# Chunk 0 of a gated linear attention with experts behind it: f and q in rows of two tokens, another order of loads, and a new table of offsets

## The chip, the cores and the metric

The kernel runs on one core of one Trainium2 chip. Its time is the device time of one execution in microseconds (us); the lower, the better. The engines are TensorE (PE, with the loading of weights shown apart as PEld), VectorE (DVE), ScalarE (ACT), GpSimd (POOL) and SyncE (SP), which here only issues transfers. L282 is line 282 of the kernel's source.

## The reference, cut to what matters

The inputs are q, k, v and f_logit of shape [4, 8, 768, 48] (batch, head, token, width) in float32. Attention is a recurrence over the tokens, with one 48x48 state for each batch and head; behind it every token of 384 values goes through four experts, whose outputs are added with the weights p.

```python
f = 1.0 / (1.0 + np.exp(-f_logit))
for t in range(S):
    state = f[:, :, t, :, None] * state + np.einsum('bhd,bhe->bhde', k[:, :, t], v[:, :, t])
    y[:, :, t] = np.einsum('bhd,bhde->bhe', q[:, :, t], state)
...
x = np.ascontiguousarray(attn_out.transpose(0, 2, 1, 3)).reshape(B * S, H * D)
p = domain_probs / (domain_probs.sum(-1, keepdims=True) + 1e-09)
for e in range(E):
    h = np.maximum(x @ w1[e], 0.0)
    out += p[:, e:e + 1] * (h @ w2[e])
```

w1 is [4, 384, 1024] and w2 is [4, 1024, 384]. The output has 3072 rows of 384.

## The kernel before

**Tiling.** The 768 tokens are cut into 6 chunks of 128, and each chunk is worked on for the 4 batches b0 to b3 one after the other; a token of the chunk is a partition. Within a chunk the recurrence is written as matrix products. With G the running sum of the gate logits (-log f) over the tokens of the chunk, q is multiplied by exp(-G) and k by exp(G); the product of the two, masked to the lower triangle, times v gives y, and from the second chunk on the carried state adds its part.

**The steps of one batch.** They have these names in the plan:

- `gate1` (L311) takes exp(-f) on ScalarE, and `gate2` (L315) takes ln(1 + that), in bfloat16, into a tile whose heads are padded to 64.
- `cs` (`pe_cs`, L319) is the running sum, one matmul of 384 columns with an upper triangle of ones (`Ub`). In chunk 0 four matmuls of a single column (L322) add up the whole chunk for the state.
- `exps` takes the two exponentials on ScalarE (L339), and in chunk 0 a small third one (L341) of the chunk's totals.
- `q` and `k` are the two products (`product`, L347), on VectorE or POOL.
- `tp` (L356) turns both with eight transposes on the PE, and `ev_tp` (L272 on ScalarE, L273 on VectorE) copies the result out of PSUM. Later chunks use a transposing transfer.
- `at` (L383) is eight matmuls of 128 columns, `ev_at0` and `ev_at1` (L387, VectorE) multiply their results by the mask `mask01` and write bfloat16 (the tile `AT`).
- `y` (L398, in later chunks also L394), then `ev_y` or `ev_ys` (L370) copies it, and `xt` (L423) turns it into the experts' input x; `ev_xt` copies that.
- `kv` (L404), `ev_kv` (L411) and `sf` (L416, L419) carry the state on.

**The experts.** The first chunks do them straight: `h` (L432) is x times w1 in blocks, `relu` (L441 or L443) cuts them off, `o` (L447) multiplies by w2 and `ev_o` adds it up with p. From the second half of chunk 1 on, two experts at a time go through a scheme that saves multiplications: `hs` (L464), `relu_s` (L470 on VectorE, L472 on ScalarE), sums of blocks `s1` to `s4` (L482), seven products `p` (L501) for each pair, `ev_p` (L509) and the stores (L513). `t` (L491) makes sums of w2 once.

**What sets the order.** The class `Plan` gives every step an engine or several to choose from, a cost, a priority, the steps it depends on, and the buffers that it takes and frees. A list scheduler walks through time, gives each free engine the first step by priority that is ready, and its answer is the fixed order in which each engine's instructions are emitted. The engines then run these lists in order, each waiting for what it needs. The table `MOVES` shifts the priority of single steps, or pins them to an engine. Until the first `h` the PE gets filler matmuls on a constant tile (L873), as many as fit into the gaps of the plan.

**Loads.** SP issues the loads of f, q, k (L282), each of one batch in chunk 0, of two batches later. The values v of chunk 0 come through POOL's queue, which casts them to bfloat16 on the way (L278). The weights come through POOL's queue too (`load_w`, L291), in eleven pieces w0 to w10: the halves of w1 of experts 0 and 1 (w0 to w3), the halves of w2 of expert 0 (w4, w5), then whole matrices: w1 of expert 2, w2 of expert 1, w1 of expert 3, w2 of experts 2 and 3. The last, w10, waits for the k of chunk 1. The order of chunk 0's loads is one line, with the places of v0 and v1 in it, each held back by one of the k loads; v2 and v3 go out behind w0:

```python
v_gate, issued = [(0, "k", 1), (0, "k", 2)], []
...
for i, x in enumerate("f0 k0 q0 f1 k1 q1 f2 f3 k2 q2 v0 k3 q3 v1".split()):
```

Each such load has a packet for each token and head, 48 values of 4 bytes. `set-up` in what follows means the constants made on POOL and VectorE before the first step: the triangle (a float32 tile `U` and its copy `Ub`), the identity, a column of ones, the zeros of the padded tiles, the mask.

Of the kernel before, what the change touches and what calls it, by code (L numbers as in the profile page):

```python
# [15 lines left out]
    "k 0.2=46.8@DVE;at 0.1=35.2;ev_xt 0.0=109.8@DVE;ev_at1 0.1=70.1;ev_y 0.3=27.8@ACT;cs 1.0=11.6;at 1.1=19.4;ev_xt 1.0=-4.1@DVE;"  # L16
    "y 1.1=-37.1;ev_ys 1.2.1.1=-9.1;ev_kv 1.3=70.1;ld q2.0=-1.5;ld k2.2=0.2;ld v2.2=15.3;relu 0.0.0.0=-7.7@DVE;h 0.0.0.256=-53.5;"
    "h 0.0.4.256=16.5;o 0.0.0.1=5.7;h 0.1.3.0=25.3;o 0.0.1.1=45.6;o 0.0.3.0=67.2;o 0.1.3.1=6.9;relu 0.3.2.0=15.9@DVE;h 0.3.3.0=-4.2;"
    "h 0.3.6.0=-15.8;o 0.2.3.0=-0.7;h 0.3.7.0=377.1;o 0.2.3.1=-2.5;tp 2.3=-3.5;at 2.1=1.3;ev_ys 2.0.0.0=-60.4@ACT;xs 2.0.1=-2.5;"
    "ev_at0 2.1=-36;ev_at0 2.2=23.5;xs 2.3.0=11.1;kv 2.0=-27.5;sf 2.0.1=-9.9;sf 2.0.3=-58.7;ld f3.0=3.2;o 0.3.1.1=10.5;o 0.3.3.0=-6.7;"  # L20
    "o 0.3.3.1=-22.1;store 0.3.0=20.5;h 1.1.3.0=2.6;o 1.0.1.1=-1;h 1.2.4.0=8.1;h 1.2.5.0=43.5;h 1.3.0.0=-9.1;o 1.2.0.0=19.1;"
    "relu 1.3.1.0=-6.8@ACT;o 1.2.1.0=1.8;h 1.3.3.0=10.5;relu 1.3.7.0=7@DVE;hs 1.1.1.0.0=-39.6;hs 1.1.1.0.4=-28.6;egs 3.1=26.2;"
    "tp 3.1=-56.1;q 3.2=2.6;ev_at0 3.1=7.2;ev_ys 3.1.0.1=20.9;ev_kv 3.0=13.3;kv 3.2=18.7;kv 3.3=10.8;ld q4.0=-7;ld k4.2=14.4;"
    "p 1.1.1.5=-1.3;ev_p 1.1.1.5=-31.6;store 1.2.0=32.2;p 1.1.1.4=5.8;s1 2.0.0=-10.2;hs 2.0.1.0.0=7;relu_s 2.0.1.0.4=1.8@ACT;"
    "p 2.0.0.4=-14.9;s1 2.0.1=2.2;hs 2.1.0.0.0=-31.7;ev_p 2.0.1.1=-60.4;ev_p 2.0.1.2=4.7;hs 2.1.0.0.2=-47.5;relu_s 2.1.0.1.2=2.4@ACT;"
    "hs 2.1.0.0.4=0.4;p 2.0.1.7=10.9;ev_p 2.0.1.3=-15.8;hs 2.1.0.1.6=-2.8;s1 2.1.0=-39.4;s2 2.1.0=2.3;p 2.1.0.1=1.8;p 2.1.0.2=56.5;"
    "ev_p 2.1.0.6=-15.4@DVE;p 2.1.0.5=-1.9;hs 2.1.1.1.6=-3;relu_s 2.1.1.1.6=9.4@DVE;s3 2.1.1=-18;cs 4.0=-6.9;egs 4.0=1.1;q 4.0=0.6;"
    "v 4.1=-4.6;tp 4.1=-14.2;cs 4.2=-65.6;cs 4.3=-4.7;ev_ys 4.0.0.1=-2.9@DVE;ev_ys 4.1.1.0=-89;ev_ys 4.2.1.1=0@ACT;ev_at0 4.3=55.1;"
    "ev_kv 4.1=52.4;kv 4.2=12.3;ld k5.0=7.4;ld f5.2=7.3;ld k5.2=-22.8;hs 3.0.0.0.2=1.4;relu_s 3.0.0.0.2=0@ACT;p 2.1.1.6=17.2;"
    "p 2.1.1.4=17.3;s4 3.0.0=8.2;relu_s 3.0.1.1.0=31.3@DVE;ev_p 3.0.0.2=-39.3;relu_s 3.0.1.0.2=36.2@DVE;p 3.0.0.5=2.3;hs 3.0.1.0.4=2.5;"  # L30
    "relu_s 3.0.1.1.4=8.8@ACT;p 3.0.0.4=3.4;hs 3.0.1.1.6=-5.6;relu_s 3.0.1.1.6=-12.6@DVE;p 3.0.1.1=7.7;hs 3.1.0.1.0=4.3;p 3.0.1.2=0.6;"
    "hs 3.1.0.0.4=-3.5;hs 3.1.0.1.6=2.1;s1 3.1.0=-4.1;s2 3.1.0=-28.8;s3 3.1.0=13.5;hs 3.1.1.0.0=0.4;relu_s 3.1.1.0.0=0@DVE;"
    "hs 3.1.1.1.0=-32.5;hs 3.1.1.1.2=5.9;relu_s 3.1.1.0.4=6.7@DVE;s1 3.1.1=10.8;s2 3.1.1=-19.8;gate1 5.2=-24.6;cs 5.2=-43.5;cs 5.3=10.3;"
    "ev_at0 5.0=-17.9;ev_at1 5.0=-18.3;ev_ys 5.0.0.0=0.1@DVE;ev_ys 5.0.0.1=18.3@DVE;ev_ys 5.1.0.0=-2.7@DVE;ev_ys 5.1.1.0=31.5@DVE;"
    "ev_at1 5.3=45.4;hs 4.0.0.0.0=23.1;hs 4.0.0.1.0=2;hs 4.0.0.0.4=-0.9;hs 4.0.0.1.4=-2.8;p 3.1.1.3=31;hs 4.0.0.0.6=-1.9;"
    "hs 4.0.0.1.6=-58.1;s2 4.0.0=6.2;hs 4.0.1.0.0=24.8;hs 4.0.1.1.0=-11.5;ev_p 4.0.0.7=-23.6;hs 4.0.1.0.6=-26.6;ev_p 4.0.0.4=2.3@DVE;"
    "hs 4.0.1.1.6=49.8;hs 4.1.0.0.2=-81.9;s1 4.1.0=-16.7;s2 4.1.0=-21.4;s4 4.1.0=-5.2;ev_p 4.1.0.1=-31.4@DVE;hs 5.0.1.1.2=15.3;"
    "hs 5.0.1.0.4=-23.8;hs 5.1.0.0.2=40.5;hs 5.1.0.1.4=9.9;hs 5.1.1.1.6=18;p 5.1.0.5=15.2"
# [3 lines left out]
class Op:  # L42


    def __init__(self, name, costs, emit, prio, deps=(), takes=(), frees=(), lag=0.0):
        self.name, self.costs, self.emit, self.prio = name, costs, emit, prio
        self.deps = [d for d in deps if d is not None]
        self.takes, self.frees, self.lag = list(takes), list(frees), lag
        self.end = self.start = self.engine = None
        self.pad = 0  # L50
        self.port, self.turn = False, None


class Plan:
# [37 lines left out]
    def run(self):  # L92
# [3 lines left out]
        for o in self.ops:  # L96
            if o.name.split(" ")[-1].startswith("0.") and set(o.costs) & {"ACT", "DVE"}:
                o.lag += 0.1
# [41 lines left out]
def kernel(  # L140
# [11 lines left out]
    nc = tc.nc  # L152
# [36 lines left out]
    U = const.tile([T, T], FP32)  # L189
    make_upper_triangular(nc, U, val=1.0, diag=True)  # L190
    Ub = const.tile([T, T], BF16)
    nc.gpsimd.tensor_copy(out=Ub, in_=U)
    ident = const.tile([T, T], BF16)
    make_identity(nc, ident)
    ones = const.tile([T, 32], BF16, name="ones")[:, 0:1]
    nc.gpsimd.memset(ones, 1.0)
    pads = {}
    for nm, nb in (("gp", 2), ("qk", 2)):
        for i in range(rooms[nm]):
            t = pads[nm, i] = const.tile([T, nb, H, P2], BF16, name=f"{nm}{i}")  # L200
            nc.vector.memset(t[:, :, :, D:P2], 0.0)
    for i in range(rooms["e"]):
# [710 lines left out]
```

## Time and profile before

| | |
|---|---|
| median of 3 runs | 289.22 us (288.99 to 289.73) |
| the profiled execution | 288.44 us |
| its span, first to last instruction | 286.7 us |
| granted TensorE clock | 1.000 |
| PE busy | 280.0 us, 98% of the span, 3010 matmuls |
| VectorE, ScalarE, POOL busy | 195.5, 180.7, 112.0 us |
| transferred | 41.85 MB in 157782 packets, 148124 of them under 512 bytes |

The page of the profile gives totals over the span and the span in 40 slices. Engines that are busy less than the whole span may still be what the others wait for in one stage, so the stages are read one by one: a view of windows gives each engine's busy time between two moments, the chain of waits says what ended last before each piece of the path, and the timeline of one engine lists its operations with the idle time ahead of them and what ended it. A row of the timeline reads: start, duration, engine, line, operation, output and inputs, count, and in square brackets the idle time before it and the releaser.

### The profile page before, as it was taken

To read this page: it belongs to the slowest core of one execution; us is meant where nothing else is said; L and a number is where in the kernel's file an instruction comes from. 1 tells how busy PE (TensorE), PEld (TensorE's weight loads), DVE (VectorE), ACT (ScalarE), POOL (GpSimd) and SP (SyncE) were. 2 spreads that over 40 slices of the span, in tenths; PEclk is the share of its full clock that TensorE was granted. 3 is DMA by queue.
4 is the path that set the end of the run, shared out by engine and by line. 5 is a ranking of instruction groups with operands and counts; after the bars stand their busy time and mean duration, and the time that the engine had idled before them with its cause. 6 is when DMAs were issued, how large, how long until landed. Compare 5 with 4: busy or idle time off the path is not lost.

```text
span 286.7 us, 7475 instructions
## 1 busy us (share of the span) xinstructions
PE 280.0 (98%) x3010; PEld 235.7 (82%) x3016; DVE 195.5 (68%) x385; ACT 180.7 (63%) x343; POOL 112.0 (39%) x181
## 2 busy tenths in 40 slices
PE   7999999999999999999999999999999999999994
PEld 2567555567786999998999999999999999998994
DVE  4595122778698868846889876888885787630683
ACT  5847683758776846867695657375865544659500
POOL 5796500218763762478157258134373000000000
PEclk9999999999999999999999999999999999999999
DMA  7999999997998989999889999995254143420011
GB/s 154 206 173 206 207 195 201 181 198 167 176 184 161 213 154 211 128 222 195 177 182 171 126 219 179 222 184 112 58 132 90 28 84 83 88 56 2 2 55 55
DMA packets 157782, 41.85 MB, mean 146 GB/s; under 512 B 148124, under 2 KB 156956, under 8 KB 157748
## 3 DMA queue, kind: packets, MB, share of 16 engines
q1 hardware_dynamic: 146500, 34.66, 63.7%
q0 software_dynamic: 11248, 6.72, 16.5%
q8 instruction: 23, 0.38, 0.6%
q14 instruction: 11, 0.09, 0.1%
HBM read 31.51 MB, written 4.72 MB: 126 GB/s over the span
## 4 chain that ended last, share of the span: by engine, by line
PE 93%; SPq 2%; DMA 2%; DVE 1%; issue 0%; ACT 0%; DVEq 0%
PE ps_m L464 33%; PE ps_m L501 29%; PE ps_m L447 11%; PE ps_m L432 11%; SPq L282 2%; PE ps_m L383 2%; PE ps_m L398 2%; DMA q<-in_q_dram 2%; PE ps_m L394 1%; PE ps_m L404 1%; PE ps_m L319 1%; PE ps_m L356 1%; DVE AT L387 0%; ACT QK L272 0%; PE ps_m L423 0%
## 5 line engine op out<-in xcount | busy, mean ns | idle before, releaser
L464 PE MATMUL ps_m<-x,w_sb 128*128 128x256 bf16 x864 | 105.6, 273 | 0.0
L472 ACT ACTIVATE h<-ps_m 128x512 bf16<-128x512 f32 x113 | 67.2, 598 | 45.3 <-PE ps_m L464 35.9
L464 PEld LDWEIGHTS <-w_sb 128*128 128x128 bf16 x864 | 82.9, 98 | 9.1
L501 PEld LDWEIGHTS <-S 128*128 128x128 bf16 x576 | 48.6, 98 | 1.1
L509 DVE TENSOR_TENSOR o<-ps_m,o 128x192 f32<-128x192 f32 x91 | 31.2, 354 | 20.0 <-PE ps_m L501 17.7
L482 DVE TENSOR_TENSOR S<-h 128x1024 bf16<-128x1024 bf16 x36 | 28.2, 800 | 13.0 <-ACT h L472 12.9
L501 PEld LDWEIGHTS <-h 128*128 128x128 bf16 x432 | 36.3, 98 | 0.9
L447 PE MATMUL ps_m<-w_sb,h 128*128 128x384 bf16 x192 | 36.1, 326 | 0.0
L432 PE MATMUL ps_m<-x,w_sb 128*128 128x128 bf16 (+2 forms) x260 | 35.6, 281 | 0.2
L443 ACT ACTIVATE h<-ps_m 128x512 bf16<-128x512 f32 (+1 forms) x49 | 24.6, 512 | 14.0 <-PE ps_m L432 12.9
L387 DVE TENSOR_TENSOR AT<-ps_m,mask 128x512 bf16<-128x512 f32 x48 | 30.5, 683 | 4.1 <-PE ps_m L383 3.8
L419 POOL TENSOR_TENSOR Sf<-Sf,egs 48x192 f32<-48x192 f32 x40 | 20.7, 521 | 28.4 <-DVE Sf L411 23.9
L339 ACT ACTIVATE e<-ps_m 128x384 f32<-128x384 f32 x48 | 26.9, 671 | 6.3 <-PE ps_m L319 2.9
L470 DVE TENSOR_SCALAR h<-ps_m 128x512 bf16<-128x512 f32 x31 | 21.0, 691 | 12.9 <-PE ps_m L464 10.3
L432 PEld LDWEIGHTS <-w_sb 128*128 128x128 bf16 x264 | 21.8, 98 | 9.4
L347 POOL TENSOR_TENSOR qk<-q,e 128x384 bf16<-128x384 f32 x19 | 24.1, 1271 | 13.7 <-ACT e L339 6.3
L501 PE MATMUL ps_m<-ts_sb,S 128*128 128x192 bf16 x288 | 28.7, 246 | 0.0
L501 PE MATMUL ps_m<-w_sb,S 128*128 128x192 bf16 x288 | 28.5, 246 | 0.0
L501 PE MATMUL ps_m<-w_sb,h 128*128 128x192 bf16 x288 | 28.4, 246 | 0.0
L447 PEld LDWEIGHTS <-h 128*128 128x128 bf16 x192 | 18.3, 98 | 11.9 <-issue 0.4
L370 ACT ACTIVATE yb<-ps_m,pn 128x384 bf16<-128x384 f32 x49 | 26.1, 584 | 2.8 <-PE ps_m L398 2.7
L347 POOL TENSOR_TENSOR qk<-k,e 128x384 bf16<-128x384 f32 x19 | 19.4, 1023 | 14.7 <-DVE Sf L411 4.0
(74 smaller groups left out, 308.7 us busy)
## 6 DMA issues: line engine op xcount, KB each, us to landing
out_dram<-o SPq DMA_DIRECT2D x23, 192.0 KB, 2.2
w_sb<-in_moe_w_dram POOLq DMA_DIRECT2D x5, 768.0 KB, 17.3
k<-in_k_dram SPq DMA_DIRECT2D x10, 384.0 KB, 5.5
q<-in_q_dram SPq DMA_DIRECT2D x10, 384.0 KB, 5.6
v<-in_v_dram SPq DMA_DIRECT2D x10, 384.0 KB, 5.6
f<-in_f_logit_dram SPq DMA_DIRECT2D x9, 384.0 KB, 4.9
w_sb<-in_moe_w_dram POOLq DMA_DIRECT2D x6, 384.0 KB, 8.7
f<-in_f_logit_dram SPq DMA_DIRECT2D x6, 192.0 KB, 3.8
```

Source lines behind the costliest of these rows:

```text
L339: nc.scalar.activation(out=o, in_=i, func=AF.Exp, scale=1.0 if j else -1.0)
L347: return engines[eng].tensor_tensor(out=tl("qk", c, b)[:, j, :, 0:D].rearrange("t (i r) d -> t i r d", r=2), in0=tl("qk"[j], c, b // 2)[:, ...
L370: nc.scalar.activation(out=ys, in_=y, func=AF.Copy, scale=pe)
L387: nc.vector.tensor_tensor(out=tl("AT", c, b)[:, r].rearrange("s i t -> s (i t)"), in0=tl("A", c, b, r).rearrange("s i t -> s (i t)"), in1= ...
L432: nc.tensor.matmul(out=hp(c, e, fc, n0, n1, nf)[:, f], lhsT=w1_sb[:, e, kk, (fc + f) * 128:(fc + f + 1) * 128], rhs=tl("xT", c)[:, kk, n0: ...
L443: nc.scalar.activation(out=dst, in_=src, func=AF.Relu)
L447: nc.tensor.matmul(out=tl("op", c, e, nt, part)[:, cols], lhsT=tl("h", c, e, half_of(c, nt * T))[:, fc, nt * T:(nt + 1) * T], rhs=w2_sb[:, ...
L464: nc.tensor.matmul(out=out_[:, f], lhsT=w1_sb[:, e, kk, (fc + f) * 128:(fc + f + 1) * 128], rhs=tl("xs", c, hf, p)[:, el, kk, :], start=(k ...
L472: nc.scalar.activation(out=dst, in_=tl("hp", c, hf, p, el, fc), func=AF.Relu)
L482: return nc.vector.tensor_tensor(out=s(j), in0=in0, in1=in1, op=op)
L501: nc.tensor.matmul(out=out_, lhsT=lhs[:, fc, :], rhs=rhs[:, fc, :], start=(first and fc == 0), stop=(fc == KF - 1), skip_group_check=True)
L509: nc.vector.tensor_tensor(out=o, in0=src, in1=o, op=ALU.add)
```

## The change

- f and q of chunk 0 are loaded with two consecutive tokens in one row: partition 2p+g holds the tokens 2p and 2p+1 for the heads of group g, so a packet has 384 bytes, and a load half as many of them. The eight loads concerned are named by `PAIRED`. k and v stay as they were.
- The running sum of chunk 0 is made twice, since q and k now lie differently. `pe_cs`, for k, is four matmuls of 192 columns with a new constant `Up`, and eight single-column ones with the constant `par`. The new `pe_cq`, for q, is four matmuls of 192 columns with `Wp`, in a PSUM tile of its own (`cq`). The exponential of q (`expq`) is a step of its own. The q product writes the padded tile by group, and the masked matmul (`pe_at`) reads its right side and writes its result with a stride, so that the tokens stand in order again.
- The set-up makes `par` (a reduction on VectorE), `Up` (four selects on POOL) and `Wp` (two copies on VectorE); `U` and its copy are gone, `Ub` is made directly, and the mask is bfloat16 instead of float32.
- The order of chunk 0's loads is written in `ORDER`, that of the v loads and weights in `SEQ`, what holds v0 and v2 back in `GATE`. The emitted order on SP is f0, q0, the probabilities, f1, f2, k0, q1, k1, f3, k2, q2, q3, k3; on POOL v0 (behind f1), v1, v2 (behind k2), the product k of b2, w0, v3, w1 and the further pieces.
- All of `MOVES` is replaced. Among the rest, the first load of chunk 2's f is now emitted on SP ahead of the last q and v loads of chunk 1.
- The plan's extra 0.1 of lag for chunk 0's steps moves into the class `Op`, and a few costs are set anew.

```diff
...
-    "k 0.2=46.8@DVE;at 0.1=35.2;ev_xt 0.0=109.8@DVE;ev_at1 0.1=70.1;ev_y 0.3=27.8@ACT;cs 1.0=11.6;at 1.1=19.4;ev_xt 1.0=-4.1@DVE;"
...
+    "ld k0.0=1.9;ld f0.2=-2.8;ld q0.2=5.3;ld q0.3=33.8;ld k0.3=74.5;w 5=-5.3;exps 0.0=4.4;ev_tp 0.0=12.5@ACT;cs 0.1=-7.1;expq 0.2=68;"
...
-    U = const.tile([T, T], FP32)
-    make_upper_triangular(nc, U, val=1.0, diag=True)
-    Ub = const.tile([T, T], BF16)
-    nc.gpsimd.tensor_copy(out=Ub, in_=U)
...
+    par = const.tile([T, 32], BF16, name="par")[:, 0:2]
+    nc.vector.tensor_reduce(out=par, in_=ident.rearrange("c (p g) -> c g p", g=2), axis=mybir.AxisListType.X, op=ALU.max)
+    Up = const.tile([T, 2, 2, T], BF16)
+    Wp = const.tile([T, 2, T], BF16)
+    for j in range(2):
+        for g in range(2):
+            nc.gpsimd.affine_select(out=Up[:, j, g], in_=par[:, g:g + 1].broadcast_to([T, T]), compare_op=ALU.is_ge, fill=0.0,
+                                    base=g - j, channel_multiplier=-1, pattern=[[1, T]])
+    Ub = const.tile([T, T], BF16)
+    nc.gpsimd.memset(Ub, 1.0)
+    nc.gpsimd.affine_select(out=Ub, in_=Ub, compare_op=ALU.is_ge, fill=0.0, base=0, channel_multiplier=-1, pattern=[[1, T]])
...
+    for j in range(2):
+        nc.vector.tensor_copy(out=Wp[:, j].rearrange("c (p g) -> c g p", g=2),
+                              in_=Up[:, j].rearrange("c g (p i) -> c g p i", i=2)[:, :, :, 0])
...
-    mask01 = const.tile([T, NP * T], FP32)
+    mask01 = const.tile([T, NP * T], BF16)
...
-            if b < 2:
-                after(ins[c, nm, b], ins[v_gate[b]])
+            if f"v{b}" in GATE:
+                after(ins[c, nm, b], ins[GATE[f"v{b}"]])
+            return
+        if c == 0 and nm in PAIRED:
+            src = {"f": f_logit, "q": q}[nm][b, :, 0:T, :].rearrange("(g h) (p j) d -> p g h (j d)", g=2, j=2)
+            ins[c, nm, b] = nc.sync.dma_start(out=tl(nm, c, b // 2)[:, hh(b), :].rearrange("t (h j) d -> t h (j d)", j=2), in_=src)
             return
...
     def gate2(c, b, n):
         g = tl("gp", c, b // 2).rearrange("t b h d -> t (b h) d")
+        if c == 0:
+            nc.scalar.activation(out=g[:, hh(b), 0:D].rearrange("t (j h) d -> t h j d", j=2),
+                                 in_=tl("f", c, b // 2)[:, hh(b), :].rearrange("t (h j) d -> t h j d", j=2), func=AF.Ln, bias=1.0)
+            return
...
-        nc.tensor.matmul(out=cs[:, 0:HD], lhsT=Ub, rhs=g[:, :, 0:D], start=True, stop=True)
-        if c == 0:
-            for i in range(NP):
-                nc.tensor.matmul(out=cs[:, HD + i:HD + i + 1], lhsT=flat(g, i), rhs=ones, start=True, stop=True)
+        if c > 0:
+            nc.tensor.matmul(out=cs[:, 0:HD], lhsT=Ub, rhs=g[:, :, 0:D], start=True, stop=True)
+            return
+        for r in range(2):
+            for j in range(2):
+                nc.tensor.matmul(out=cs[:, r * HD // 2:(r + 1) * HD // 2], lhsT=Up[:, j, r], rhs=g[:, 4 * j:4 * j + 4, 0:D],
+                                 start=(j == 0), stop=(j == 1), skip_group_check=True)
+        for i in range(NP):
+            for j in range(2):
+                nc.tensor.matmul(out=cs[:, HD + i:HD + i + 1], lhsT=flat(g, j * 2 + i % 2), rhs=par[:, i // 2:i // 2 + 1],
+                                 start=(j == 0), stop=(j == 1), skip_group_check=True)
+
+    def pe_cq(b):
+        g, cs = tl("gp", 0, b // 2)[:, b % 2], tl("cq", 0, b)
+        for r in range(2):
+            for j in range(2):
+                nc.tensor.matmul(out=cs[:, r * HD // 2:(r + 1) * HD // 2], lhsT=Wp[:, int(j > r)], rhs=g[:, 4 * j:4 * j + 4, 0:D],
+                                 start=(j == 0), stop=(j == 1), skip_group_check=True)
...
         if c == 0:
+            nc.scalar.activation(out=tl("e", c, b)[:, 2 * NP * P2:], in_=cs[:, 0:HD], func=AF.Exp, scale=1.0)
             nc.scalar.activation(out=tl("egs", c, b)[0:MP, 0:NP], in_=cs[0:MP, HD:HD + NP], func=AF.Exp, scale=-1.0)
+
+    def expq(b):
+        nc.scalar.activation(out=tl("e", 0, b)[:, 0:HD], in_=tl("cq", 0, b)[:, 0:HD], func=AF.Exp, scale=-1.0)
...
+        if (c, j) == (0, 0):
+            return engines[eng].tensor_tensor(out=tl("qk", c, b)[:, 0, :, 0:D].rearrange("t (j h) d -> t j h d", j=2),
+                                              in0=tl("q", c, b // 2)[:, hh(b), :].rearrange("t (h j) d -> t j h d", j=2),
+                                              in1=tl("e", c, b)[:, 0:HD].rearrange("t (j h d) -> t j h d", j=2, d=D), op=ALU.mult)
...
+                if c == 0:
+                    qt = QK[rows, 0].rearrange("m (j i) (p g) -> m i g p j", i=2, g=2)[:, i % 2, i // 2]
+                    a = a.rearrange("t (p j) -> t p j", j=2)
+                nc.tensor.matmul(out=a, lhsT=QK[rows, 1, i, :], rhs=qt, start=True, stop=True)
...
+PAIRED = "fq"
+ORDER = "f0 q0 k0 f1 q1 k1 f2 f3 q2 k2 q3 k3"
+SEQ = "v0 v1 v2 w0 v3 w1"
+GATE = {"v0": (0, "f", 1), "v2": (0, "k", 2)}
+LATE = {}
```

## The prediction

> **What bounds the kernel now.** I read the page first: the row of granted clock says one speed throughout, and the PE row is full from the third of 40 slices on. Then the stages:
>
> ```profile
> span 286.7 us, 7475 instructions
> ...
> PE   7999999999999999999999999999999999999994
> ...
> PEclk9999999999999999999999999999999999999999
> ```
>
> ```profile
> core 0: us, PE busy (x) PEld busy (x) DVE busy (x) ACT busy (x) POOL busy (x), PEclk, DMA share, GB/s
> 0.00:20.38 20.38, 17.50 (x164) 9.62 (x166) 12.75 (x28) 12.22 (x28) 14.59 (x29) 1.00 1.23 176
> 20.38:283.20 262.82, 262.51 (x2847) 226.03 (x2851) 182.19 (x357) 168.50 (x317) 97.45 (x153) 1.00 0.78 144
> 283.20:286.70 3.50, 0.00 (x0) 0.00 (x0) 0.57 (x2) 0.00 (x0) 0.00 (x0) 1.00 0.24 84
> ```
>
> From 20.38 to 283.2 the PE idles 0.31 us; before that much of its busy time is filler (matmuls of L873 on a constant tile, 32 in the records). After it come 3.5 us of last sums and stores. So the time is: when chunk 0's attention hands the PE its work, plus a fixed amount of matmuls, plus whatever waits a new order puts in, plus the tail. What sets 20.38 is in the chain of waits and in VectorE's timeline:
>
> ```profile
> 8.20 4.64 DMA q<-in_q_dram
> ...
> 12.93 0.57 DVE qk L347
> ...
> 17.16 1.08 ACT QK L272 x2
> ...
> 19.03 1.30 DVE AT L387 x2
> ...
> 20.38 0.35 PE ps_m L398 x7
> ```
>
> ```profile
> 10.10 1.28 DVE L387 TENSOR_TENSOR AT<-ps_m,mask 128x512 bf16<-128x512 f32 x2
> 12.93 0.56 DVE L347 TENSOR_TENSOR qk<-q,e 128x384 bf16<-128x384 f32 x1 [1.55 <-DMA q<-in_q_dram]
> 13.40 0.55 DVE L347 TENSOR_TENSOR qk<-k,e 128x384 bf16<-128x384 f32 x1
> ...
> 16.59 1.88 DVE L387 TENSOR_TENSOR AT<-ps_m,mask 128x512 bf16<-128x512 f32 x3
> ...
> 19.03 1.29 DVE L387 TENSOR_TENSOR AT<-ps_m,mask 128x512 bf16<-128x512 f32 x2 [0.30 <-PE ps_m L398]
> ```
>
> The third batch's q lands at 12.84, VectorE waits 1.55 us for it, then works nearly without a stop to 20.32: loads to 12.9, VectorE from there. Steps below are "b0" to "b3", the batches of chunk 0.
>
> **The change, part by part.**
>
> *Loads.* In the window 3 to 7 us queue 1 moved 4569 packets, all of 192 bytes, at a share of 111.3% of 16 engines: 1.113 x 16 x 4.0 / 4569 = 15.6 ns each, so 1024 of them take 1.0 us of the 16 engines. Rows of two tokens make 512 packets of 384 bytes. The trace has no such packet. The stores between 280 and 287 us average 47 ns at 1024 bytes (432 packets, 16.6%, the 48 small ones taken off at 8 ns); a line through both gives 23 ns for 384 bytes, an estimate, 0.73 us a load. Bounds: 31 ns (two small ones, nothing gained) and 15.6 ns (half the time). Eight loads (f and q) at 0.27: 2.1 us less in the stream, with 0 and 4.0 as ends. f of b0 lands at 3.25 rather than 3.52. The values v0 and v1 now go out once f1 is in (about 5.4 to 7.2 on POOL, 1.06 and 0.95 each) instead of at 7.61 and 11.42, and share the engines with q1 to k3. Between 9 and 12 us the one v load cost the others about 0.8 us, so k3, now the last, lands near 14, against 14.87 for the last q before. It is needed at 15.4 (below): loads stop being what VectorE waits for.
>
> *ScalarE.* Per batch two gates (0.53, 0.52), two exponentials (0.87 for two), one small (0.18): the same five, in another order. Nothing.
>
> *TensorE before the masks.* Per batch one 384-column matmul and four of one column become eight of 192 and eight of one. Early matmuls start 0.43 us apart for 512 columns, 0.16 for 192; later 0.21, and 0.083 for 192 (L501 rows: 8 in 0.66). Single columns take 0.065 (3 weight loads in 0.20). So cq is 0.64 then 0.35, cs 1.15 then 0.85. In program order from the end of gate2 b0 (3.25 + 1.1 = 4.35): cq0 0.64, cs0 1.15, the four transposes of the probabilities 0.8, a filler 0.3 (7.25); cs1 0.85, tpq0 0.22, cq1 0.35, filler 0.21, tpk0 0.22, cq2 0.35, cs2 0.85, filler, tpk1, filler, tpq1 0.9: 11.2. With 0.15 of latency and the copy of QK1 on VectorE (0.6; it starts back-to-back operations that much apart) the first mask AT0 begins at about 12.0; I take 12.2 for the joins. Ends: 11.4 (the array fast from the start) and 13.7 (a rival).
>
> *VectorE from there.* AT0 1.22, q2 0.47, AT1 1.22, q3 and k3 0.94, the copy of y0 0.42, AT2 1.22, x0 0.30, half of AT3 0.61, x1 0.30, the other half 0.61: 7.3 us, to 19.5, when the y of b3 may start; it ends at 19.9. Before it ended at 20.73. The copy of x1 stands at 18.9 in this list, so the PE has by 19.9 also done the h block of b1 (0.65) and the transposes of b2 (0.15), which before came after 20.73. Gain: 0.83 + 0.65 + 0.15 = 1.6 us. POOL now multiplies one k only (0.99 to 1.00 each before), beside VectorE operations that read PSUM. The bf16 mask is read beside f32 from PSUM: taken as no change, at best 0.05 each.
>
> *Set-up.* POOL has four selects of 0.29 and two operations on Ub instead of U's two and its cast: it ends near 5.4 instead of 3.9. Its first user is v0, gated by f1 at 4.8: 0.6 late, needed at 15. VectorE adds a reduction (0.25) and two copies (0.23) and is ready at 5.1; its first product is due at 5.8. If that cover went, each 0.1 would move the product, which has 0.5 to spare before k0.
>
> *Weights.* The first piece now stands in POOL's queue behind v2's issue (gated by k2, near 11) and the product of k2 (needs exps2, 11.0): issued near 13 instead of 12.37. Behind it wait v3 and all other pieces. Before, v1 landed at 15.93 and this piece 2.4 us later; now three v are through by about 15, so it lands at 17.3 (18.33 before). Its user, h of b0, can start at 18.1. The second piece lands near 19.9 (21.79), wanted at 20.6. Later pieces follow 1.9 us apart, 1.9 us earlier than before, and the PE wants them 1.6 earlier. Cost nothing; covers of 0.8 and 0.7 us.
>
> *New offsets.* From 20.4 on the PE's instructions are the same in another order. At most the 0.31 idle can go; at the other end every wait in an in-order queue counts in full. I take 0: counted over the new order, blocks stand behind the operations that feed them about as before.
>
> *Tail.* Two sums of the last-but-one pair's group now come last and one more store of 192 KB: 0.2 (0 to 0.7), from 0.36 for an issue and 0.31 for a sum.
>
> Sum: -1.6 + 0 + 0.2 = -1.4. The profiled execution took 288.44 with a span of 286.7, and stands 0.78 below the median of 289.22; the difference goes on both: span 285.3, 287.0 for a like execution, 287.8 for the median.
>
> **The rivals.**
>
> *A, more.* The single-column matmuls and the early ones run faster than I put them, AT0 starts at 11.4, and the new order saves the idle 0.3: -2.5, 286.7. For it: three single-column weight loads show 0.20 while the array is slow. Against: the PE list then must have no join in it.
>
> *B, the array stays slow.* The row of granted clock shows 1.00 from the start, yet L873 starts 0.43 us apart until 6.8 and 0.21 apart later. The new program has 21 fillers instead of 34, and single-column matmuls in their place. If the switch comes late, the column time of cs1 to tpq1 doubles: (0.64 + 0.64 + 0.85 + 0.6) = 2.8 us at most, about 1.4 if it comes half-way. AT0 then starts at 13.6 and the gain is gone: 289.2. Against: the PE still has work from 1.5 us on. The Trainium skill, page "TensorE: Matmul & The Clock Gate", section "Part 1: The HAM clock gate", has the array at half clock until one free-running window of about 3.4 us was busy; by that rule the switch comes at a window's end, near 6.9 or, missed, 3.4 us later, which is this rival; the trace agrees on the factor of two and not in the granted-clock row.
>
> *C, slower: a late weight piece in the dense stage.* The last piece (w2 of expert 3) waits for chunk 1's k, issued at 49.59, landed 9.1 us later at 58.67; its matmuls began at 59.79. They now come up near 58.2. SyncE's list has a 384 KB load more (chunk 2's f, 2048 packets, 2.0 us) ahead of chunk 1's last q and v, in just that stretch. If the pieces do not move earlier and this load goes ahead, it lands at 60.7, a stall of 2.5: +1.1, 290.3. It turns the sign once it lands after 59.6. Against: everything ahead of it on the engines is 2.1 us less, so 56.6 is as good a guess, and the load waits for a buffer. The same price holds wherever the new order meets a late operand.
>
> **How the numbers follow.** The likeliest, 287.8 (own range 287.0 to 288.7): 0.46. A 0.18, B 0.14, C 0.22. 0.3% is 0.87 us, about what a measurement of this kernel can tell from no change. Faster takes A and nine tenths of the likeliest: 0.59. Same: the rest of it and most of B: 0.17. Slower: C and a little of B: 0.24. Range 286.0 to 290.8: below A by the 0.7 that packets at 15.6 ns could add, above C by the tail's upper end.
>
> **What would show it.** Right: queue 1 in the first 12 us at about 23 ns for a packet; no wait of VectorE for a load after 6 us; AT0 near 12.2 and unbroken work behind it to 19.5; two h blocks before the y of b3; PE idle from there to the end below 0.7 us. Wrong: AT0 after 13 with early matmuls still 0.16 apart for 192 columns (B); a PE gap over 0.5 us beside a weight piece's landing (C) or behind another engine; a first h block that waits for its weights; a tail over 4 us.

## The result, and the profile after

The changed kernel takes 290.14 us (median of 20 runs, 289.42 to 291.50), the kernel before 289.05 (20 runs beside them, 288.27 to 290.63): a ratio of 1.0039, 95% interval 1.0027 to 1.0052. It is slower by 1.1 us, where 1.4 us less was forecast. The profiled execution took 289.52 us, with a span of 287.7. The page, and the stages in the view of windows, cut where the y of b3 ends (22.55) and where the last matmul ends (283.80):

```profile
span 287.7 us, 7539 instructions
...
PE   6999999999999999999999999999999999999994
...
PEclk9799999999999999999999999999999999999999
```

```profile
core 0: us, PE busy (x) PEld busy (x) DVE busy (x) ACT busy (x) POOL busy (x), PEclk, DMA share, GB/s
0.00:22.55 22.55, 19.55 (x221) 13.48 (x222) 14.40 (x34) 13.32 (x28) 15.58 (x32) 0.92 1.14 170
22.55:283.80 261.25, 261.25 (x2829) 224.98 (x2826) 182.72 (x363) 164.82 (x304) 96.58 (x153) 1.00 0.81 143
283.80:287.70 3.90, 0.00 (x1) 0.00 (x0) 0.62 (x2) 0.00 (x0) 0.00 (x0) 1.00 0.41 151
```

The kernel before, cut at the same two events:

```profile
0.00:20.73 20.73, 17.85 (x173) 9.97 (x176) 13.10 (x28) 12.57 (x28) 14.94 (x29) 1.00 1.23 177
20.73:283.11 262.38, 262.16 (x2840) 225.68 (x2841) 181.78 (x356) 168.15 (x316) 97.10 (x153) 1.00 0.78 144
283.11:286.70 3.59, 0.00 (x0) 0.00 (x0) 0.62 (x2) 0.00 (x0) 0.00 (x0) 1.00 0.24 82
```

The y of b3 ends 1.82 us later. The second stage is 1.13 shorter. Of that, 0.84 is work that the changed kernel has done by the cut and the kernel before has not: a second h block (0.67) and the transposes of b2 (0.17). Another 0.22 is idle time of the PE, which is gone (262.38 less 262.16 before, none after), and 0.07 is left over. The tail is 0.31 longer. 1.82 - 1.13 + 0.31 is the 1.0 us between the spans: **the loss is in the first 22.5 us**, and in the other 265 the idle time saved and the longer tail come out about even.

VectorE's timeline there (start, duration, operation, idle time before it and its releaser) answers to the one shown of before:

```profile
9.59 0.56 DVE L388 TENSOR_TENSOR qk<-k,e 128x384 bf16<-128x384 f32 x1 [1.05 <-DMA k<-in_k_dram]
...
12.64 0.69 DVE L280 COPY QK<-ps_m 112x1024 bf16<-112x1024 bf16 x1 [1.94 <-PE ps_m L397]
13.36 1.29 DVE L431 TENSOR_TENSOR AT<-ps_m,mask 128x512 bf16<-128x512 f32 x2
...
18.47 1.29 DVE L431 TENSOR_TENSOR AT<-ps_m,mask 128x512 bf16<-128x512 f32 x2 [0.76 <-PE ps_m L428]
...
20.33 0.69 DVE L431 TENSOR_TENSOR AT<-ps_m,mask 128x512 bf16<-128x512 f32 x1 [0.30 <-PE ps_m L428]
...
21.20 0.68 DVE L431 TENSOR_TENSOR AT<-ps_m,mask 128x512 bf16<-128x512 f32 x1
```

The first mask begins at 13.36 (10.10 before, 12.2 forecast), the last ends at 21.88 (20.32 before, 19.5 forecast), and from 10.7 on the waits are for the PE. The page's row of the clock has a 7 in its second slice, 7.2 to 14.4 us. Windows of 1 us there (the last three columns are granted clock, DMA share and GB/s):

```profile
7.00:8.00 1.00, 0.40 (x5) 0.38 (x4) 0.58 (x2) 1.00 (x5) 1.00 (x2) 0.92 1.15 266
8.00:9.00 1.00, 1.00 (x17) 0.97 (x16) 0.54 (x1) 0.97 (x4) 0.49 (x1) 0.50 1.15 233
9.00:10.00 1.00, 1.00 (x8) 0.71 (x6) 0.41 (x1) 0.81 (x3) 0.00 (x0) 0.50 1.89 181
10.00:11.00 1.00, 1.00 (x10) 0.95 (x9) 0.70 (x2) 0.70 (x2) 0.00 (x0) 0.50 1.57 177
11.00:12.00 1.00, 1.00 (x18) 0.87 (x16) 0.00 (x0) 0.68 (x2) 0.00 (x0) 0.87 2.01 182
```

The granted clock is 0.50 from about 7.8 to 11.3. The array had been fast before that: from 5.11 on it starts four matmuls of 192 columns in 0.33 us, from 8.68 on in 0.63. Ahead of the slow stretch the PE stood idle twice: from 4.26 to 5.11, since its fillers ended and the first f landed at 3.96 instead of 3.52, and for 0.60 before cs1. A third thing stands in the PE's timeline: the eight masked matmuls of a batch take 0.72 instead of 0.40.

```profile
12.54 0.72 PE L428 MATMUL ps_m<-QK 48*128 48x128 bf16 x8
13.94 0.71 PE L428 MATMUL ps_m<-QK 48*128 48x128 bf16 x8
17.72 0.71 PE L428 MATMUL ps_m<-QK 48*128 48x128 bf16 x8
19.58 0.71 PE L428 MATMUL ps_m<-QK 48*128 48x128 bf16 x8
```

### The profile page after: what moved, and what is told of

It reads as the page before. It is cut to its first block, busy times and chain, and to the rows that moved or that the text cites. A ratio compares the mean times of both kernels' runs of the same rounds, so it can differ in the third digit from the quotient of the medians.

```text
span 287.7 us, 7539 instructions
## 1 busy us (share of the span) xinstructions
PE 280.8 (98%) x3047; PEld 238.5 (83%) x3047; DVE 197.7 (69%) x398; ACT 178.1 (62%) x332; POOL 112.2 (39%) x184
## 4 chain that ended last, share of the span: by engine, by line
PE 96%; DMA 1%; SPq 1%; ACT 0%; issue 0%; DVE 0%; DVEq 0%
PE ps_m L508 33%; PE ps_m L545 29%; PE ps_m L476 11%; PE ps_m L491 11%; PE ps_m L428 3%; PE ps_m L442 2%; PE ps_m L438 1%; PE ps_m L923 1%; PE ps_m L448 1%; DMA f<-in_f_logit_dram 1%; PE ps_m L397 1%; PE ps_m L339 1%; PE ps_m L354 1%; PE ps_m L343 1%; SPq L291 0%; PE ps_m L467 0%
## 5 line engine op out<-in xcount | busy, mean ns | idle before, releaser
L516 ACT ACTIVATE h<-ps_m 128x512 bf16<-128x512 f32 x111 | 66.2, 598 | 45.0 <-PE ps_m L508 36.0
L463 POOL TENSOR_TENSOR Sf<-Sf,egs 48x192 f32<-48x192 f32 x40 | 22.9, 573 | 50.8 <-DVE Sf L455 33.4
L526 DVE TENSOR_TENSOR S<-h 128x1024 bf16<-128x1024 bf16 x36 | 26.7, 762 | 15.0 <-ACT h L516 13.9
L411 ACT ACTIVATE yb<-ps_m,pn 128x384 bf16<-128x384 f32 x50 | 26.7, 583 | 9.9 <-PE ps_m L442 8.3
L388 POOL TENSOR_TENSOR qk<-q,e 128x384 bf16<-128x384 f32 x18 | 21.5, 1195 | 22.9 <-ACT e L372 15.3
L487 ACT ACTIVATE h<-ps_m 128x512 bf16<-128x512 f32 (+1 forms) x44 | 22.7, 525 | 12.3 <-PE ps_m L476 11.2
L514 DVE TENSOR_SCALAR h<-ps_m 128x512 bf16<-128x512 f32 x33 | 22.5, 689 | 8.5 <-PE ps_m L508 8.0
L545 PE MATMUL ps_m<-w_sb,h 128*128 128x192 bf16 x288 | 27.5, 246 | 0.0
L372 ACT ACTIVATE e<-ps_m 128x384 f32<-128x384 f32 x40 | 23.4, 709 | 3.7 <-PE ps_m L339 2.6
```

Source lines behind the costliest of these rows:

```text
L372: nc.scalar.activation(out=o, in_=i, func=AF.Exp, scale=1.0 if j else -1.0)
L388: return engines[eng].tensor_tensor(out=tl("qk", c, b)[:, j, :, 0:D].rearrange("t (i r) d -> t i r d", r=2), in0=tl("qk"[j], c, b // 2)[:, ...
L411: nc.scalar.activation(out=ys, in_=y, func=AF.Copy, scale=pe)
L463: return nc.gpsimd.tensor_tensor(out=Sf[rows, b], in0=Sf[rows, b], in1=eg, op=ALU.mult)
L516: nc.scalar.activation(out=dst, in_=tl("hp", c, hf, p, el, fc), func=AF.Relu)
L526: return nc.vector.tensor_tensor(out=s(j), in0=in0, in1=in1, op=op)
```

## The experiments

All ratios are to the kernel before, run beside each on the same chip; 0.001 of the ratio is 0.29 us.

**1. Three suspects, one at a time.** e1_warm adds fillers (`EXTRA = {"cq 0.0": 2, "cs 0.1": 1}`):

```diff
-        for _ in range(o.pad):
+        for _ in range(o.pad + EXTRA.get(o.name, 0)):
```

> The changed kernel with three fillers more: two ahead of cq0, one ahead of cs1, where its PE stands idle for 0.85 us (4.26 to 5.11) and 0.60 us (7.02 to 7.62). Theory 1, the idle array: the two gaps keep the array at half speed until 11.4 (granted clock 0.50 from 8 to 11 us, where the kernel before has 1.00 from the start); without them it is fast from about 7, the PE's 3.1 us of work between 8.3 and 11.4 take half, at0 starts near 11.1 instead of 12.54, AT0 near 11.9 instead of 13.36, and the time falls by 1.0 to 1.5 us, to 288.6 to 289.1. Theory 2, the strides in the masked matmuls, and theory 3, the late first f (3.96 instead of 3.52), leave this kernel where it is: 290.1, AT0 within 0.3 of 13.36.

e2_flat takes the reordering out of the masked matmuls, and e3_mix does so batch by batch:

```diff
-                if c == 0:
-                    qt = QK[rows, 0].rearrange("m (j i) (p g) -> m i g p j", i=2, g=2)[:, i % 2, i // 2]
-                    a = a.rearrange("t (p j) -> t p j", j=2)
```

> The changed kernel with the masked matmuls of chunk 0 on plain operands: the step that puts q's tokens back in order is left out, so the tokens of chunk 0 stay permuted and the mask falls on the wrong ones; all else is the same work. Theory 2: the eight matmuls take 0.40 as before instead of 0.72, four times, and since three of the four stand between VectorE's masks and the copies they wait for, the time falls by 0.6 to 1.3 us (288.8 to 289.5). Theory 1 and theory 3: only the one ahead of AT0 counts, 0.3 at most (289.8 to 290.1).

> One look for durations: in chunk 0 the masked matmuls of b0 on plain operands, of b1 with only q read at a stride, of b2 with only the result written at a stride, of b3 with both (tokens of b0 to b2 stay permuted). If the strided read is what takes the time: 0.40, 0.72, 0.40, 0.72; if the strided write: 0.40, 0.40, 0.72, 0.72; if each takes half: 0.40, 0.56, 0.56, 0.72.

e4_unpaired has the old layout under the new order:

```diff
-PAIRED = "fq"
+PAIRED = ""
...
-        for r in range(2):
-            for j in range(2):
-                nc.tensor.matmul(out=cs[:, r * HD // 2:(r + 1) * HD // 2], lhsT=Up[:, j, r], rhs=g[:, 4 * j:4 * j + 4, 0:D],
-                                 start=(j == 0), stop=(j == 1), skip_group_check=True)
+        nc.tensor.matmul(out=cs[:, 0:HD], lhsT=Ub, rhs=g[:, :, 0:D], start=True, stop=True)
```

> The changed kernel with f and q of chunk 0 in rows of one token again, and the matmuls that go with it (one of 384 columns for q's sum, one of 384 and four single columns for k's, masked matmuls on plain operands); the order of every queue and all offsets stay those of the changed kernel. If the layout is what made it slower (theories 2 and 3, and the long chains of small matmuls on a slow array): first f lands at 3.5, AT0 begins before 12.5, and the time is 288.3 to 289.3. If the order and the offsets made it slower: 290 or more, since all 12 loads now have 1024 packets and the last k lands near 16.5 instead of 15.1.

| | median us | ratio (95%) | first mask | last mask begins |
|---|---|---|---|---|
| changed | 290.14 | 1.0039 (1.0027 to 1.0052) | 13.36 | 21.20 |
| e1_warm | 290.45 | 1.0026 (1.0005 to 1.0046) | 11.93 | 21.70 |
| e2_flat | 290.82 | 1.0044 (1.0028 to 1.0060) | 11.69 | 21.59 |
| e4_unpaired | 290.81 | 1.0048 (1.0025 to 1.0070) | 13.84 | 21.94 |

None of the three makes up the loss alone. e1_warm did to the first mask what theory 1 said (11.93, from 13.36, with the granted clock at 1.00), and the time did not follow. (Its profiled execution is the longest of its twelve, 291.38 us; a single trace shows what can happen, not how often.) The masked matmuls go back to 0.40 in e2_flat, and the time did not follow either; in its profiled execution the array happened to stay fast without fillers. The old layout does not mend anything, though its array, too, was slow until about 9.8, and its clock at 0.50 from 13.2 to 16.6. Theory 1, 2 and 3 in their simple form fall. What e1_warm ran into is on VectorE and on POOL:

```profile
14.58 1.60 DVE L385 TENSOR_TENSOR qk<-q,e 128x384 bf16<-128x384 f32 x1 [1.36 <-DMA q<-in_q_dram]
16.10 1.28 DVE L431 TENSOR_TENSOR AT<-ps_m,mask 128x512 bf16<-128x512 f32 x2
```

```profile
13.85 0.88 POOL L285 DMA_DIRECT2D vb<-in_v_dram  x1 [5.54 <-DMA k<-in_k_dram]
14.74 1.01 POOL L388 TENSOR_TENSOR qk<-k,e 128x384 bf16<-128x384 f32 x1
```

k2 landed at 13.57. v2's issue, which waits for it, takes 0.88 on POOL, and the product of k2 stands behind that issue in POOL's queue. It then runs beside VectorE's product of q2, which takes 1.60 instead of 0.55. The second mask begins at 16.10, later than in the changed kernel (15.03), and behind the masks the PE of e1 waits 0.53 us (at 24.2) and 0.57 us (at 33.1) for weight pieces. And k2 is late since v0 and v1 now share the engines with it: with both put back, in e5 below, it lands at 11.19. How late k2 is seems to depend on a race, in which v0 (released by f1) and SP's issue of f3 begin at about the same moment; that is read from these five executions and was not tested:

| | v0's issue begins | k2 lands |
|---|---|---|
| e2_flat | 6.28 | 13.77 |
| e1_warm | 6.35 | 13.57 |
| e7_kfirst_warm | 6.52 | 12.28 |
| changed | 6.53 | 12.16 |
| e3_mix | 6.71 | 12.35 |

Before, with v0 issued at 7.61 and v1 at 11.42, k2 landed at 11.13.

e3_mix, one run of 289.26 us, has 0.40, 0.71, 0.40 and 0.71 for the four batches. So the read of q takes the time. (The expectation, and the list of changes above, have the result written at a stride; in the kernel's order of columns it is written in sequence, so that half could not show anything.) The two columns of each pair of q lie 512 bytes apart there. By the Trainium skill, page "SBUF — State Buffer", section "Door 1: The DMA port swizzle", reads that step to a new line of 16 bytes each time pay a penalty; the trace agrees, 0.71 against 0.40.

**2. The values back, with and without fillers.** The emitted order of POOL is changed, and everything else kept: v0 waits for k0, v1 goes behind the product of k2, then the first weight piece, v2, v3.

```diff
     done = P.run()
+    at_ = lambda n: next(i for i, o in enumerate(done) if o.name == n)
+    for name, behind in SHIFT:
+        o = done.pop(at_(name))
+        done.insert(at_(behind) + 1, o)
...
-            if f"v{b}" in GATE:
-                after(ins[c, nm, b], ins[GATE[f"v{b}"]])
+            if f"v{b}" in EMIT_GATE:
+                after(ins[c, nm, b], ins[EMIT_GATE[f"v{b}"]])
...
+SHIFT = [("v issue 1", "k 0.2"), ("w issue 0", "v issue 1"), ("v issue 2", "w issue 0")]
+EMIT_GATE = {"v0": (0, "k", 0)}
```

> The kernel of e1_warm (fillers in the two gaps) with the loads of the values put back to about where the kernel before had them: v0 waits for k0, v1 goes out behind POOL's product of k2, then the first weight piece, v2, v3. All other lists are unchanged. In e1_warm k2 landed at 13.6 and the product of k2, which stands behind the issue of v2 on POOL, began at 14.7 and ended at 16, which the transposes of b2 waited for. Theory 4, the values ahead of the work: with one v load instead of two in the stream between 6.5 and 13.5 us, k2 lands near 12, the product ends near 13.2, VectorE's first mask of b1 starts at 13.6 instead of 16.1, and the time falls by 1 to 1.7 us against e1_warm, to 288.7 to 289.4, unless a y then waits for its late values (v2 and v3 land near 18 and 19.5). Theory 5, the order of the PE's own list (fillers, the sums of b3 ahead of the transposes of b2, the long masked matmuls): no change, 290.2 to 290.7.

> e5_vlate_warm without the three fillers. If the slow array costs time once the loads are out of the way, it is slower than e5_vlate_warm by 0.5 to 1.4 us (where the profile shows the clock at half). If something else ends last in either case, the two are equal within 0.3 us.

e7_kfirst_warm only swaps v2's issue and the product (`SHIFT = [("v issue 2", "k 0.2")]`):

> The kernel of e1_warm with one instruction moved on POOL: the issue of v2 behind the product of k2 instead of ahead of it. Theory 4 in its narrow form (the issue ahead of the product costs, the stream itself does not): the product starts with the landing of k2 instead of 1.1 us later, q2 on VectorE is not stretched to 1.6 us, and the time falls by 0.8 to 1.1 us against e1_warm. In its wide form (the stream is late) it falls by 0.5 at most. Theory 5: no change.

e8_vlate_warm_jp is e5 with another order of columns in the masked matmul:

```diff
-                    qt = QK[rows, 0].rearrange("m (j i) (p g) -> m i g p j", i=2, g=2)[:, i % 2, i // 2]
-                    a = a.rearrange("t (p j) -> t p j", j=2)
+                    qt = QK[rows, 0].rearrange("m (j i) (p g) -> m i g j p", i=2, g=2)[:, i % 2, i // 2]
+                    a = a.rearrange("t (p j) -> t j p", j=2)
```

> e5_vlate_warm with the masked matmuls reading q token half by token half (64 columns 4 bytes apart, twice) instead of pair by pair (each next column 512 bytes on); the result is written at a stride, so the tokens are in order and the output is the reference's. If it is the pair-wise read that takes 0.72 instead of 0.40: 0.40 to 0.45 each, and 0.3 to 0.9 us less than e5_vlate_warm. If any stride of the moving operand does: 0.72 still, and no gain.

| | values early | values back |
|---|---|---|
| no fillers added | changed: 1.0039 (1.0027 to 1.0052) | e6: 1.0037 (1.0024 to 1.0051) |
| fillers added | e1: 1.0026 (1.0005 to 1.0046) | e5: 1.0008 (0.9992 to 1.0025) |

This table is the answer. Each remedy alone leaves the time where it was within the intervals; together they take 0.3%, 0.9 us, off. **The slow array and the early values are two delays beside each other, and either can hide the end of the other.** The times show it for the fillers: worth 0.8 us once the values are back (e6 against e5). For the values, the 0.5 us between e1 and e5 is not clear of the intervals; the 1.3 us between e7, below, and e5 is, and the rest is read from the traces. k2 lands at 11.2 in e5 and in e6, so what holds e6 back is the array: its first mask begins at 13.01, against 11.89 in e5. e5's VectorE (timeline):

```profile
11.89 1.29 DVE L431 TENSOR_TENSOR AT<-ps_m,mask 128x512 bf16<-128x512 f32 x2
13.10 0.55 DVE L385 TENSOR_TENSOR qk<-q,e 128x384 bf16<-128x384 f32 x1
13.57 1.28 DVE L431 TENSOR_TENSOR AT<-ps_m,mask 128x512 bf16<-128x512 f32 x2
...
17.01 1.29 DVE L431 TENSOR_TENSOR AT<-ps_m,mask 128x512 bf16<-128x512 f32 x2 [0.76 <-PE ps_m L428]
...
18.87 0.69 DVE L431 TENSOR_TENSOR AT<-ps_m,mask 128x512 bf16<-128x512 f32 x1 [0.30 <-PE ps_m L428]
```

Every mask is 1.5 us earlier than in the changed kernel, the end of the y of b3 0.8. Yet e5 is no faster than the kernel before, since the next thing is late, as its PE shows:

```profile
19.63 0.37 PE L442 MATMUL ps_m<-vb,AT 128*128 128x48 bf16 x8 [0.53 <-DMA vb<-in_v_dram]
...
22.89 1.29 PE L476 MATMUL ps_m<-x,w_sb 128*128 128x128 bf16 x20 [0.43 <-DMA w_sb<-in_moe_w_dram]
```

e7 (1.0053, 1.0032 to 1.0073) gained 1.8 us on the second mask (14.30), more than either form of theory 4 said of the product, and lost it again: with the values ahead, the first weight piece came at 20.14 and the PE waited 0.71 us for it, then 0.29 for the second, 0.28 at 31.6, and 0.97 for the last, w10, which landed at 61.90. e8 (1.0016, 0.9999 to 1.0033) has masked matmuls of 0.61, not of 0.40 to 0.45, and no gain in time over e5.

**3. The supply.** e10_vhw takes the values out of POOL's queue: SP loads them in float32, ScalarE casts them. e11_vhw_trim is that with eight fillers fewer.

```diff
+        if o.name.startswith("v issue"):
+            continue
         o.ins = o.emit(o.engine)
...
+            for b in V_LOAD.get(o.name, ()):
+                nc.sync.dma_start(out=stage[b][:, hh(b), :], in_=srcs["v"][0, :, b * H:(b + 1) * H, :])
+            for b, eng in V_CAST.get(o.name, ()):
+                copy(eng, tl("vb", 0, b), stage[b][:, hh(b), :])
...
+V_LOAD = {"ld k0.2": (0,), "ld k0.3": (1, 2, 3)}
+V_CAST = {"gate2 0.3": ((0, "ACT"),), "ev_tp 0.2": ((1, "ACT"),), "ev_tp 0.3": ((2, "ACT"),), "ev_y 0.1": ((3, "ACT"),)}
```

> e8_vlate_warm_jp with the values of chunk 0 loaded in float32 by SP (v0 behind k2, v1 to v3 behind k3) and cast on ScalarE in four copies of about 0.5, instead of cast on the way by POOL's queue. Theory 6: in e5 and e8 what is left is the supply through POOL's queue (1024 packets of 96 bytes at 29 ns are 1.9 us of the engines for a v load, against 1.0 for 192-byte packets; v2 lands at 19.2 to 19.6, the first weight piece at 18.5, the second at 22.2 to 22.9, and the PE waits for them). Then the first piece lands by 17.5, the second by 19.8, the last y starts by 20, and the time is 287.6 to 288.6. Rival: the stream of SP gets longer by the same amount, k3 and the values land late, and the time stays at 289.3 or more.

> e10_vhw with eight fillers fewer where the PE's list has run ahead of the plan: two ahead of the masked matmul of b1, one ahead of y of b0, three ahead of the transpose of q of b3, two ahead of the masked matmul of b3. If fillers stand on the path, it is 0.3 to 0.8 us faster than e10_vhw; if the PE waits there anyway, it is equal; if the array falls back to half speed, slower.

303.71 and 304.09 us, 5% slower. The rival that was named said 289.3 or more; nothing of this size was expected. v1 came in time, at 16.4. But v2, issued at 12.45, landed at 26.95, and v3 at 32.31. ScalarE's timeline:

```profile
26.97 0.51 ACT L279 CAST vb<-v 128x384 bf16<-128x384 f32 x1 [8.52 <-DMA v<-in_v_dram]
```

From about 15 us on the weight pieces, packets of 1024 bytes at some 98 ns, were on the same engines. The first packets of v2 appear at about 18.5. From then on the two queues run side by side, here from 20 to 24 us (packets, MB, share of 16 engines; q0 is POOL's queue, q1 SP's):

```profile
q0 software_dynamic: 646, 0.64, 93.9%
q1 hardware_dynamic: 645, 0.12, 27.7%
```

One small packet goes with one large: 645 in 4 us on 16 engines is one in 99 ns on each engine, where alone they follow each other at 15. By the Trainium skill, page "DMA: Bandwidth & Descriptors", section "Queues, rings and completion order", each engine takes turns between its queues packet by packet; the trace agrees in kind, 645 against 646. Why v2 moved nothing before 18.5 stays open.

e12_novalues and e13_before_novalues leave the four loads out, to see what they cost, and e16 repairs e13:

```diff
-            ins[c, nm, b] = nc.gpsimd.dma_start(out=tl("vb", c, b), in_=srcs[nm][c, :, b * H:(b + n) * H, :])
+            nc.gpsimd.memset(tl("vb", c, b), 1.0)
+            return
...
+        if i == 0:
+            after(ins["w", i], ins[0, "q", 2])
```

The first three lines are in all of them (e12 is e8 with them), the last two in e16 alone.

> e8_vlate_warm_jp with the four loads of chunk 0's values left out: the tiles are filled with ones on POOL instead (so the output isn't the reference's); all other work is there. Theory 6, the supply: what keeps e5 and e8 at the time of the kernel before is that the values (7.6 us of POOL queue's packets) now delay k3, two of the y and the second weight piece. Then k3 lands by 14.5 (16.3 in e8), the last y starts near 19.2 to 19.8, the weights land 3 us earlier, and the time is 287.0 to 288.2. If the chain of operations bounds the prologue by itself, 289 or more.

> The kernel before with the same four loads left out in the same way (output not the reference's). The values' cost in the order of the kernel before: v0 stood beside q2 (about 0.8 us of it). If theory 6 holds, taking the values away is worth less here than in e12_novalues against e8: 288.2 to 288.9, a gain of 0.3 to 1.0; if it is worth as much, the values were as much in the way before, and their new place isn't the cause.

> e13_before_novalues with the first weight piece held until q2 has landed, which puts its issue back to about 12.4 (the values are left out, so the output isn't the reference's). Theory 6: the values cost the kernel before 0.3 to 1.0 us (v0 beside q2), 288.2 to 288.9, less than the 1.2 us that they cost e8. If 287.8 or less, their new place is not what differs.

e12: 288.20, 0.9968 (0.9952 to 0.9984), 1.4 us below e8 by the ratios. e13: 1.0036 (1.0006 to 1.0067), with runs from 288.6 to 295.3, is a control that went wrong: its first weight piece went out at 10.1 instead of 12.4, and q3, issued at 10.25, landed at 17.98, as the loads of e10 did beside weights (VectorE's timeline):

```profile
18.00 0.56 DVE L348 TENSOR_TENSOR qk<-q,e 128x384 bf16<-128x384 f32 x1 [2.61 <-DMA q<-in_q_dram]
```

e16, with that piece held to its old place: 288.09, 0.9968 (0.9951 to 0.9985). Without values the new front and the old one take the same time. So the values cost the kernel before 0.9 us (0.4 to 1.4 by the interval), at the upper end of what was expected, and e8 1.4; a difference of 0.5 is not clear of the intervals. Theory 6 holds in that the values cost time in both, and fails in that it is not shown to be their new place, once the array is fast and POOL's order mended.

e14_vhalf and e15_vhalf_trim keep the whole computation, with v0 and v1 through SP and v2 and v3 behind the first weight piece on POOL:

> e8_vlate_warm_jp with v0 and v1 loaded in float32 by SP (behind k2 and behind k3) and cast on ScalarE, while v2 and v3 stay in POOL's queue behind the first weight piece. In e10_vhw the loads of SP up to v1 came in time (v1 at 16.4) and only v2 and v3, which the weight pieces overtook, were late (27 and 32). If the supply through POOL's queue is what is left, the first piece lands near 17.5 to 18.5, v2 near 18.5, the second piece near 21, and the time is 288.0 to 288.8, below e8 and the kernel before. If not, 289.0 or more.

> e14_vhalf with the eight fillers fewer of e11_vhw_trim. If fillers stand on the path between the masks and the y, 0.2 to 0.6 us faster than e14_vhalf; if loads end last there, equal.

e14: 288.81, 0.9993 (0.9976 to 1.0011); e15: 288.61, 0.9989 (0.9971 to 1.0007). They are the best of the complete kernels, 0.5% below the changed one, and not shown to be faster than the kernel before. Whether the fillers of e15 stood on the path cannot be told from 0.04%.

## Why the prediction was wrong

**The step that failed** is the one that the gain came from: "the first mask AT0 begins at about 12.0; I take 12.2", and VectorE "to 19.5" behind it. Measured: 13.36, and 8.5 us instead of 7.3 to the end of the last mask. So of the sum, the 0.83 that the y of b3 was to end earlier became 1.82 later; the other two terms, 0.65 + 0.15 for the block and the transposes, held (0.84).

- *The array.* The list of the PE took the array to be fast from 7.25 on: cs1 to the last transposes of b1 were to take 3.95 us, to 11.2. They began at 7.62 and took 5.0. A slow array was rival B, at 0.14, with 13.6 for the first mask, but not by this way: B has the switch to full speed come late, and here it came early, by 5.1 (near 7 in the kernel before), and the array fell back at 7.8. B's figure for the mask is close in part by luck. B as written is seen in the traces of e6 and e15. Of the five profiled executions without the added fillers (changed, e2, e3, e4, e6) four had the array at half speed for 1.5 us or more between 8 and 11 us, by either way; of the nine with them (e1, e5, e7, e8, e10, e11, e12, e14, e15) one, e15. The prediction held against B that "the PE still has work from 1.5 us on". That is not so: f0 was put at 3.25 and landed at 3.96, and the fillers had been laid out by a plan that did not know it. I should have counted fillers against the landing. B's time, 289.2, was too low: e6, which has the slow array without the early values, stands at 1.0037, 290.1.
- *f0.* "f of b0 lands at 3.25 rather than 3.52" has the wrong sign. A packet of 384 bytes took 23 to 26 ns (23 forecast, about right; of the 4569 packets behind the 15.6 ns, 70 were of 4 bytes, which changes it by 0.1). But SP needs 0.74 for the issue, not 0.45, the first packet starts at 2.31 instead of 1.91, and from there SP's issues, 0.62 each, seem to set the pace: the DMA share is 0.63 between 4 and 5 us, where it was 1.09 before. Cheaper packets bring nothing in a stretch in which the engines wait for the next issue.
- *The masked matmuls.* They appear in the change as a stride and have no term in the sum at all. They take 0.31 more each, 1.2 of the PE's time in all; VectorE's wait of 0.76 for the third batch's is gone in e2_flat. No run shows that they cost the kernel time. The read at 512 bytes was in the diff, and a row of the same shape at unit stride (0.40) was at hand as a lower bound.
- *The values.* Taken as 0.8 us for the others ("Between 9 and 12 us the one v load cost the others about 0.8") and k3 at "near 14". That size is confirmed by e16 for one v (q2 lands at 12.00 without it, 12.84 with). Two of them made k3 15.1 (17.0 in e1), and "loads stop being what VectorE waits for" did not hold: VectorE waits 1.05 us for a k at 9.59 in the changed kernel, 1.36 for the third q in e1.
- *POOL's queue.* v2's issue ahead of the product of k2 was named, and priced only for the weight piece behind them (13 forecast, 14.28 measured). Who waits for the product itself, which is the transposes of b2, was not followed.
- *Weights.* Forecast to land at 17.3 and 19.9, the first two pieces landed at 19.23 and 22.09. The covers of 0.8 and 0.7 were gone, and only the late masks hid it. e1, e5 and e7 show it as soon as the masks are earlier.
- *Right:* set-up and ScalarE's operations at nothing, two h blocks ahead of the y of b3, little from the offsets in the dense stage (0.22 of idle time saved, where 0 to 0.31 was allowed), no stall at the last weight piece (58.83 against 58.67; rival C did not occur in the changed kernel, though its place is where e7 lost 0.97), and the tail's 0.2, measured 0.31.

The time lies inside the stated range, 286.0 to 290.8, on the side that was given 0.24. That C's 290.3 is near the measured 290.14 is luck: C's late piece did not occur. What was missing is a rival of two delays together; each of mine had one.

What stays open: with array, order and supply mended (e12 against e16) the new front should have been 1.6 us ahead by the prediction's sum and is level. In e12 the first mask begins at 11.80, where the kernel before does it at 10.10, in the time that it waits for q2 anyway; the waits of 0.55 and 0.30 for the masked matmuls are still there, and so is one of the PE, 0.25, for the second weight piece. Taking those away one by one was not tried.

## What to carry to other kernels

When a change removes a wait, list everything that ends within a microsecond of it, and mend all of them at once in an experiment: here each remedy alone measured as nothing, and a study that stopped there would have cleared both causes. On an in-order queue, an instruction that waits for the same event as its successor (v2's issue and the product of k2) puts its own duration on the successor's path. And a load that is early on one queue is paid for by those on the other, so an early place for it is worth asking about only where the engines have time to spare.

## What the hardware did that was not expected

- The array's clock fell back to 0.50 for about 3.4 us (7.8 to 11.3) after idle times of only 0.85 and 0.60, in a stretch in which the PE was otherwise busy. It did so in e3_mix too (idle 0.83 and 0.80), and not in e2_flat (0.87 and 0.33). By the Trainium skill, page "TensorE: Matmul & The Clock Gate", section "Part 1: The HAM clock gate", one idle window of about 3.4 us throttles it; the length agrees, but there was no idle time of that length here. In e6 and e15 the array was as slow until 10.4 and 10.9 with the clock row at 1.00, so that row alone doesn't tell it; the spacing of equal matmuls does (four of 192 columns in 0.64 or in 0.33).
- A moving operand in which the two columns of each pair lie 512 bytes apart takes 0.71 for eight matmuls of 128 columns, against 0.40. Read in runs of 64 columns 4 bytes apart and written to PSUM at a stride of 8 bytes, it takes 0.61.
- Two operations of 384 columns on VectorE and POOL at once took 1.60 on VectorE, where one alone takes 0.55.
- Beside packets of 1024 bytes on one queue, a load's 192-byte packets on another came one for each of them: one in 99 ns on an engine, instead of 15 (e10, 20 to 24 us).
